# First stage of an attention and two MoE kernel: order of transfers, row tiles, value products and weight conversion rearranged

## The chip, the cores and the metric

The kernel runs on one core of one Trainium2 chip. The metric is the device time of one execution in microseconds (us). PE is TensorE (matrix products), DVE is VectorE, ACT is ScalarE, POOL is GpSimd, and SP is SyncE, which issues nearly all transfers. Each engine works through its own instructions in program order, and waits on semaphores for the others.

## The reference

Three layers in a row on 2304 tokens (4 batches of 576 positions): attention with 8 heads of 64, a first MoE layer with a leaky activation, and a second one with a bounded one. Cut to what is computed:

```python
# attention: q, k, v [4, 8, 576, 64], s [4, 8, 576]
scores = q @ k.T / sqrt(64)
cum = cumsum(maximum(s, 0), axis=-1)
scores = where(causal, -1e9, scores + minimum(-(cum[:, None] - cum[None, :]), 0))
attn = exp(scores - max(scores))
x = (attn / (sum(attn) + 1e-9)) @ v            # [2304, 512] after the heads are joined
# MoE 1: w_in [512, 2048], w_out [2048, 512], alpha [2048]
h = x @ w_in
x = (maximum(h, 0) + alpha * minimum(h, 0)) @ w_out
# MoE 2
h = x @ w_in2
out = (h * clip(h + 3, 0, 6) / 6) @ w_out2
```

Everything is float32. The kernel keeps that precision with products of split values: a high part that PE takes at full rate, and the rest as a second number (names end in h and l, or hi and lo).

## The kernel before

The work stands in one program with three kinds of stages. In the first stage (L663 to L673) PE does attention for the first 256 positions of batches 0 and 1: 16 heads, taken as 8 pairs. In the second (L674 on) it does the first MoE layer for those 512 tokens, one f-step at a time, and between the steps more attention: the first 256 positions of batches 2 and 3, another 8 pairs by the same code. The rest of attention, the rest of MoE 1 and all of MoE 2 come after that.

A head of the first kind has these steps. `scores` (L508) puts products into one PSUM bank, by `softmax_a` (L243): the score products and, for pairs 0 and 1, products that add the running sums of `s` with selection matrices (`pick`, `cum2`). For the other pairs the running sums stand in four extra rows of the operands (`Rows`, L472): the key tile has the sums in its first two rows and ones below, the query tile the reverse, so that one product gives score and bias. DVE then adds the mask and takes the minimum in two passes (L262), ACT takes exponentials (L267), DVE the reciprocal of the sum (L268, L269), and POOL scales (L271). PE transposes the result in three pieces (L518), ACT copies it to SBUF (L519), and PE multiplies it with the values (L525, L526). After each second head ACT and DVE split the outcome into `xhi` and `xlo` (L530, L531), which are MoE 1's input. `attention0` (L533) runs the heads with a lag of one: the transposes of a head come after the scores of the next one.

`cumulate` (L220) makes the running sums: load `s`, scale it on DVE (L227), a scan on DVE that adds a zero tile (L231; POOL fills the zeros, L229), the split (L237, L240), a write to the DRAM tensor `cum_scratch` (L241), from which each pair's four rows are read back (L502, L503). The rows have three pairs of tiles in turn, which POOL fills ahead of time with -1 and 1 (L480, L481).

`keep_clock` (L463) issues products of a constant tile `busy` whose result nobody reads: 18 at the start, and two after the transposes of every head of the first stage.

MoE weights come in eight units of four tiles of 128x512 float32. `load_unit` (L115) issues a unit's transfers from SP. `split_part` (L131) converts: per tile ACT scales (L146), POOL bounds and rounds in two passes (L148, L151), DVE assembles the bits in two passes (L156, L159), ACT copies the high part (L162), DVE subtracts for the low part (L163). `W_LD` and `W_AT` (L28, L29) give the step of attention at which a unit is loaded or converted in the first stage; that conversion has a raised priority (`WP0`). A scheduler places the instructions of each engine by priority, except where `keep_in_program_order` fixes them.

The second stage begins with MoE 1's product h (L186) for f = 0 and 1. ACT and DVE then form the activation (L611 and L612, name gt), its split follows, and two steps later the second product y (L589). There are two PSUM banks for h, so f = 2 waits for the activation of f = 0.

Of the kernel before, what the change touches and what calls it, by code (L numbers as in the profile page):

```python
# [9 lines left out]
F32 = mybir.dt.float32  # L10
# [5 lines left out]
P = 128  # L16
# [11 lines left out]
W_LD = (8, 11, 14)  # L28
W_AT = (2, 14)  # L29
# [31 lines left out]
def attention_moe_moe(ctx, tc, qt, kt, qn, kn, vp, s, w_in1, w_out1, alpha, w_in2, w_out2, out):  # L61
# [158 lines left out]
    def cumulate(pool, first):  # L220

        s_sb = pool.tile([P, S], F32, tag="wcv", bufs=WB0, name="s_sb")
# [18 lines left out]
        nc.sync.dma_start(cum_d.rearrange("t b s -> (t b) s"), cum2[:D].bitcast(F32))  # L241
# [230 lines left out]
    class Rows:  # L472


        def __init__(self, pool, n):
            self.tiles = []
            for i in range(n):
                k = pool.tile([P, 2, NA], F32, name=f"kr{i}")
                q = pool.tile([P, 2, NA], F32, name=f"qr{i}")
                nc.gpsimd.memset(k[:R], -1.0)  # L480
                nc.gpsimd.memset(q[:R], 1.0)  # L481
                self.tiles.append((k, q))

    class Pair:
# [5 lines left out]
        def load(self, pool):  # L490
            i, self.pool = self.i, pool
            if i < 2:
                self.k = pool.tile([P, NA], F32, tag="kraw", name="kraw")
                nc.sync.dma_start(self.k, kn[i, :, :NA])
                self.q = pool.tile([P, NA], F32, tag="qraw", name="qraw")
                nc.sync.dma_start(self.q, qn[i, :, :NA])
            else:
                self.k, self.q = pool.rows.tiles[i % 3]
                both = slice(2 * i, 2 * i + 2)
                nc.sync.dma_start(self.k[R : R + D], kt[both, :D, :NA].rearrange("j d n -> d j n"))  # L500
                nc.sync.dma_start(self.q[R : R + D], qt[both, :D, :NA].rearrange("j d n -> d j n"))
                nc.sync.dma_start(self.k[: R // 2], cum_d[:, both, :NA])  # L502
                nc.sync.dma_start(self.q[R // 2 : R], cum_d[:, both, :NA])  # L503
            self.v = pool.tile([P, 2, 2, D], F32, tag="vraw", bufs=3, name="vraw")
            for j in range(2):
                nc.sync.dma_start(self.v[:, j], vp[2 * i + j, :, :2, :])
# [14 lines left out]
        def values(self, j):  # L521
            if j == 0:
                self.pv = bank("pv")
            js = slice(j * D, (j + 1) * D)
            nc.tensor.matmul(self.pv[js, :NA], self.v[:, j, 0, :], self.pT[j][:, :NA], start=True, stop=False)  # L525
            nc.tensor.matmul(self.pv[js, P:NA], self.v[:, j, 1, :], self.pT[j][:, NA:], start=False, stop=True)  # L526
            if j == 1:
                b, pr = divmod(self.i, H // 2)
                xh, xl = xblock(b)
                nc.scalar.activation(xh[:, pr, :], self.pv[:, :NA], AF.Copy)  # L530
                nc.vector.tensor_tensor(xl[:, pr, :], self.pv[:, :NA], xh[:, pr, :].bitcast(F32), op=ALU.subtract)  # L531

    def attention0(pool, pairs, lag, together):  # L533
# [301 lines left out]
```

## Time and profile before

| what | value |
|---|---|
| median of 3 runs | 1028.53 us (1028.15 to 1029.7) |
| the profiled execution's own time | 1028.13 us |
| its span, first to last instruction | 1026.4 us |
| mean granted TensorE clock | 0.993 of full |
| busy: PE / DVE / ACT / POOL | 1004.1 / 535.6 / 593.6 / 389.0 us |
| end of the first stage on PE, first h product | 53.56 us |

The profile comes from one execution. A busy share is an average over stages, so the stretches matter more than the whole: PE has work nearly all the time from 68 us on, and the gaps lie before that. Idle time of an engine is listed with the instruction whose end released it.

### The profile page before, as it was taken

Reading aid. Unit: us, or ns where it says so; the run is one execution under the profiler, and the core shown is the slowest. Engines: PE = TensorE matmul, PEld = TensorE weight load, DVE = VectorE, ACT = ScalarE, POOL = GpSimd, SP = SyncE. Lnnn points to the kernel's source line nnn. Section 1 sums busy time; section 2 is a strip of 40 time slices with the busy share of each in tenths; the row PEclk is TensorE's granted clock in tenths of the full one; section 3 lists DMA queues with packets and bytes.
Section 4 is the critical chain, followed back from the end, with each engine's and each line's share of the span. In section 5 each row is a group of like instructions: output and inputs, shape, how many; then the busy total and the mean of one; then the engine's idle time right before and its main releaser. Section 6 shows DMA issues by size and latency. Waiting matters only on the chain.

```text
span 1026.4 us, 16686 instructions
## 1 busy us (share of the span) xinstructions
PE 1004.1 (98%) x5858; PEld 866.1 (84%) x5858; DVE 535.6 (52%) x1357; ACT 593.6 (58%) x1326; POOL 389.0 (38%) x535
## 2 busy tenths in 40 slices
PE   6989999999999999999999999999999999999998
PEld 3668878999999999998998888887888888888897
DVE  4669873466666666657644873555322322322222
ACT  4768867678778778778745753665322422422232
POOL 6566737667667666757531630331000000000000
PEclk8999999999999999999999999999999999999999
DMA  5581405113122222222106654000200100000010
GB/s 174 183 288 55 175 4 164 43 39 94 51 85 61 75 63 84 68 78 75 33 27 202 230 201 150 39 0 1 82 1 1 62 1 1 25 17 1 1 42 21
DMA packets 47578, 76.84 MB, mean 75 GB/s; under 512 B 4824, under 2 KB 25480, under 8 KB 47496
## 3 DMA queue, kind: packets, MB, share of 16 engines
q1 hardware_dynamic: 47496, 75.79, 22.7%
q8 instruction: 46, 0.75, 0.3%
q14 instruction: 36, 0.29, 0.1%
HBM read 66.18 MB, written 9.58 MB: 74 GB/s over the span
## 4 chain that ended last, share of the span: by engine, by line
PE 92%; ACT 2%; DVE 2%; DMA 1%; POOL 1%; issue 1%; SPq 0%; ACTq 0%; POOLq 0%; DVEq 0%
PE y L589 19%; PE h L786 19%; PE h L186 19%; PE o L759 13%; PE o L762 6%; PE s L344 4%; PE pv L406 4%; PE pt L381 3%; PE s L256 1%; DMA wraw<-in_w_out 1%; PE pt L518 1%; PE pv L525 1%; ACT t L267 0%; DMA wraw<-in_w_in 0%; DMA qr<-in_qt 0%
## 5 line engine op out<-in xcount | busy, mean ns | idle before, releaser
L186 PE MATMUL h<-xhi,wi 128*128 128x256 f32 (+1 forms) x896 | 225.1, 321 | 2.7 <-DVE gt L612 2.1
L786 PE MATMUL h<-yhl,wi 128*128 128x512 f32 (+1 forms) x960 | 213.2, 370 | 0.2
L786 PEld LDWEIGHTS h<-yhl,wi 128*128 128x128 f32 x960 | 169.3, 188 | 34.7 <-DVE gt L789 1.1
L186 PEld LDWEIGHTS h<-xhi,wi 128*128 128x128 f32 x896 | 155.9, 190 | 16.6 <-DVE gt L612 3.6
L589 PE MATMUL y<-gh,wo 128*128 128x256 f32 (+1 forms) x896 | 166.4, 317 | 0.0
L788 ACT ACTIVATE gt<-h,three 128x512 f32<-128x512 f32 (+1 forms) x80 | 51.7, 646 | 166.9 <-PE h L786 163.3
L789 DVE SCALAR_TENSOR_TENSOR gt<-gt,h 128x512 f32<-128x512 f32 (+1 forms) x80 | 50.7, 634 | 183.7 <-ACT gt L788 183.3
L759 PE MATMUL o<-wo,gh 128*128 128x512 f32 x576 | 145.8, 391 | 0.1
L589 PEld LDWEIGHTS y<-gh,wo 128*128 128x128 f32 x896 | 134.0, 190 | 11.0 <-issue 0.3
L186 PE MATMUL h<-xlo,wi 128*128 128x256 f32 (+1 forms) x448 | 142.2, 318 | 0.0
L759 PEld LDWEIGHTS o<-wo,gh 128*128 128x128 f32 x576 | 106.8, 188 | 22.9 <-ACT gh L792 0.9
L148 POOL TENSOR_SCALAR wcv<-wcv 128x512 f32<-128x512 f32 x64 | 48.8, 767 | 154.5 <-ACT wcv L146 152.9
L589 PE MATMUL y<-gl,wo 128*128 128x256 f32 (+1 forms) x448 | 91.1, 316 | 0.0
L186 PEld LDWEIGHTS h<-xlo,wi 128*128 128x128 f32 x448 | 85.4, 191 | 6.0 <-issue 0.2
L793 DVE TENSOR_TENSOR gl<-gt,gh 128x512 fp32r<-128x512 f32 (+1 forms) x80 | 51.1, 639 | 69.1 <-ACT gh L792 45.5
L356 POOL TENSOR_SCALAR t<-t,rec 128x384 f32<-128x384 f32 (+2 forms) x96 | 65.7, 685 | 53.2 <-DVE rec L355 25.8
L347 DVE CUSTOM_DVE_ANT_0 t<-s,mask 128x384 f32<-128x384 f32 (+2 forms) x96 | 54.0, 564 | 58.4 <-PE pt L381 40.0
L792 ACT ACTIVATE gh<-gt 128x512 fp32r<-128x512 f32 (+1 forms) x80 | 47.2, 591 | 64.0 <-DVE gt L789 32.9
L612 DVE SCALAR_TENSOR_TENSOR gt<-gt,beta,h 128x256 f32<-128x256 f32 (+1 forms) x112 | 61.5, 550 | 40.4 <-ACT gt L611 39.5
L762 PE MATMUL o<-wo,gl 128*128 128x512 f32 x288 | 79.8, 390 | 0.0
L589 PEld LDWEIGHTS y<-gl,wo 128*128 128x128 f32 x448 | 70.1, 190 | 6.2 <-issue 0.2
L352 ACT ACTIVATE t<-t,m 128x384 f32<-128x384 f32 (+2 forms) x96 | 67.2, 700 | 7.2 <-DVE m L347 6.7
(109 smaller groups left out, 1669.4 us busy)
## 6 DMA issues: line engine op xcount, KB each, us to landing
wraw<-in_w_in SPq DMA_DIRECT2D x32, 512.0 KB
wraw<-in_w_out SPq DMA_DIRECT2D x32, 512.0 KB
kraw<-in_kt SPq DMA_DIRECT2D x32, 288.0 KB
qraw<-in_qt SPq DMA_DIRECT2D x32, 160.0 KB
vraw<-in_vp SPq DMA_DIRECT2D x32, 160.0 KB
y_scratch<-yt SPq DMA_DIRECT2D x18, 256.0 KB
yr<-y_scratch SPq DMA_DIRECT2D x4, 1024.0 KB
out<-ot SPq DMA_DIRECT2D x16, 256.0 KB
```

The costliest lines, as they stand in the source:

```text
L186: nc.tensor.matmul(dst, lt, r, start=first and i == 0, stop=last and i == len(terms) - 1)
L347: nc.vector.tensor_tensor_reduce(t[:n, a:e], sc[:n, : e - a], mask[:n, MASK + n - (e - a) :][:, : e - a] if e == w else mask[:n, : e - a], ...
L352: nc.scalar.activation(t[:n, :w], t[:n, :w], AF.Exp, bias=m[-1][:n], scale=-1.0, accum_out=den[:n])
L356: nc.gpsimd.tensor_scalar(t[:n, :w], t[:n, :w], rec[:n], 1.0, op0=ALU.mult, op1=ALU.mult)
L589: nc.tensor.matmul(ys[dc // per][:, o : o + n], which[:, dc * P : (dc + 1) * P], gg, start=(f == 0 and which is wl and dc % per == 0), sto ...
L612: nc.vector.scalar_tensor_tensor(gt, gt, beta[:, f : f + 1], hp[:, :n], op0=ALU.mult, op1=ALU.add)
L759: nc.tensor.matmul(op[i], lt[:, tsl], r, start=(f == 0 and r is wh), stop=False)
L762: nc.tensor.matmul(op[i], gl[:, tsl], wh, start=False, stop=(f == FC - 1))
L786: nc.tensor.matmul(hp[:, :n], lt, r, start=(i == 0), stop=(i == len(terms) - 1))
L788: nc.scalar.activation(gt[:, :n], hp[:, :n], AF.Relu, bias=three)
L789: nc.vector.scalar_tensor_tensor(gt[:, :n], gt[:, :n], 6.0, hp[:, :n], op0=ALU.min, op1=ALU.mult)
L793: nc.vector.tensor_tensor(gl[:, :n], gt[:, :n], gh[:, :n].bitcast(F32), op=ALU.subtract)
```

## The change

- The transfers of the first stage are issued in program order. First come `s`, then keys, queries and values of pairs 0 to 2 and further keys and queries, the write of the running sums, and their rows; weights follow.
- The rows stand in one tile for all six pairs 2 to 7 of the first stage (one tile for the four pair slots of the second), filled on DVE in the first stage and on POOL in the second. Two transfers bring all rows; before there were two for each pair.
- The keys and queries of pairs 0 and 1 share a tile with the weight buffers. The values of a pair come in one transfer, into four buffers in turn instead of three.
- The zero tile is one element that the scan reads again and again. `busy` is filled on DVE.
- `values` does both heads of a pair: four products in the order head 1, head 0 for the first block of keys, then the same for the second.
- The two unread products after the transposes stay for pairs 0 and 1 only: 24 go, 8 stay.
- `W_LD` and `W_AT` put a third unit's conversion into the first stage.

```diff
-W_LD = (8, 11, 14)
-W_AT = (2, 14)
+W_LD = (6, 10, 14)
+W_AT = (2, 8, 14)
...
-            nc.sync.dma_start(s_sb[part * BH : (part + 1) * BH], s)
-        first.load(pool)
+            pin(nc.sync.dma_start(s_sb[part * BH : (part + 1) * BH], s))
+        for pr in first:
+            pr.load(pool, pin)
...
-        zz = pool.tile([P, S], F32, tag="wcv", bufs=WB0, name="zz")
-        nc.gpsimd.memset(zz, 0.0)
+        zero = pool.zero
+        nc.gpsimd.memset(zero, 0.0)
...
-        nc.vector.tensor_tensor_scan(cum, sp, zz, initial=0.0, op0=ALU.add, op1=ALU.add)
+        nc.vector.tensor_tensor_scan(cum, sp, zero.to_broadcast([P, S]), initial=0.0, op0=ALU.add, op1=ALU.add)
...
-        nc.sync.dma_start(cum_d.rearrange("t b s -> (t b) s"), cum2[:D].bitcast(F32))
+        pin(nc.sync.dma_start(cum_d.rearrange("t b s -> (t b) s"), cum2[:D].bitcast(F32)))
+        pool.rows.load(pin)
...
+        def __init__(self, pool, first, n, fill):
+            self.first, self.n = first, n
+            self.k = pool.tile([P, n, 2, NA], F32, name="kr")
+            self.q = pool.tile([P, n, 2, NA], F32, name="qr")
+            fill(self.k[:R], -1.0)
+            fill(self.q[:R], 1.0)
+
+        def load(self, pin=lambda ins: ins):
+            rows = cum_d[:, 2 * self.first : 2 * (self.first + self.n), :NA]
+            for half in (self.k[: R // 2], self.q[R // 2 : R]):
+                pin(nc.sync.dma_start(half.rearrange("r n j k -> r (n j) k"), rows))
...
+        def values(self):
+            pv = bank("pv")
+            for c in range(2):
+                for j in (1, 0):
+                    i = nc.tensor.matmul(
+                        pv[j * D : (j + 1) * D, c * P : NA], self.v[:, j, c, :], self.pT[j][:, c * NA :][:, : NA - c * P],
+                        start=(c == 0), stop=(c == 1),
+                    )
+                    if c == 1 or j == 0:
+                        tc.keep_in_program_order(i)
...
-            if pr.i < H:
+            if pr.i < 2:
                 keep_clock(pr.pool.busy, 2, t)
...
-        nc.gpsimd.memset(pool.busy, 1.0)
-        att = attention0(pool, [Pair(i) for i in range(H)], LAG, 0)
+        nc.vector.memset(pool.busy, 1.0)
+        pool.rows = Rows(ahead, 2, H - 2, nc.vector.memset)
+        att = attention0(pool, [Pair(i) for i in range(H)], LAG)
```

What stands in a row on three engines shows where instructions moved. First SP, from the values of pair 2 on (kr and qr are the row tiles, wraw the weights, cum_scratch the running sums in memory), before:

```order
L506 DMA vraw<-in_vp 128x128 x2
L126 DMA wraw<-in_w_in 128x2x512
L126 DMA wraw<-in_w_out 128x1024
L241 DMA cum_scratch<-cum_109 64x576
L126 DMA wraw<-in_w_in 128x2x512
L126 DMA wraw<-in_w_out 128x1024
L500 DMA kr_111<-in_kt 64x2x256
L501 DMA qr_112<-in_qt 64x2x256
L500 DMA kr_115<-in_kt 64x2x256
L502 DMA kr_119<-cum_scratch 2x2x256
L503 DMA qr_120<-cum_scratch 2x2x256
```

and now:

```order
L510 DMA vraw<-in_vp 128x2x128
L507 DMA kr<-in_kt 64x2x256
L508 DMA qr<-in_qt 64x2x256
L243 DMA cum_scratch<-cum_109 64x576
L507 DMA kr<-in_kt 64x2x256
L508 DMA qr<-in_qt 64x2x256
L488 DMA kr<-cum_scratch 2x12x256
L488 DMA qr<-cum_scratch 2x12x256
L126 DMA wraw<-in_w_in 128x2x512
L126 DMA wraw<-in_w_out 128x1024
```

The four weight transfers stood on both sides of the write; all of them now stand behind the rows.

Then ACT at the start (t are the exponentials of one head in two pieces, wcv the weight tiles), before:

```order
L237 ACTIVATE cum2_109<-cum_163 128x576
L146 ACTIVATE wcv_246<-wraw_238 128x512
L146 ACTIVATE wcv_247<-wraw_240 128x512
L267 ACTIVATE t_191,den_193<-t_191,m_192 128x128
L267 ACTIVATE t_191,den_193<-t_191,m_192 128x256
L267 ACTIVATE t_210,den_212<-t_210,m_211 128x128
L267 ACTIVATE t_210,den_212<-t_210,m_211 128x256
L146 ACTIVATE wcv_264<-wraw_242 128x512
L267 ACTIVATE t_289,den_291<-t_289,m_290 128x128
L267 ACTIVATE t_289,den_291<-t_289,m_290 128x256
L146 ACTIVATE wcv_265<-wraw_244 128x512
L267 ACTIVATE t_320,den_322<-t_320,m_321 128x128
```

and now:

```order
L270 ACTIVATE t_201,den_203<-t_201,m_202 128x128
L270 ACTIVATE t_201,den_203<-t_201,m_202 128x256
L146 ACTIVATE wcv_230<-wraw_222 128x512
L270 ACTIVATE t_273,den_275<-t_273,m_274 128x128
L146 ACTIVATE wcv_231<-wraw_224 128x512
L523 ACTIVATE pT_213<-pt_214 128x384
L270 ACTIVATE t_273,den_275<-t_273,m_274 128x256
L146 ACTIVATE wcv_248<-wraw_226 128x512
L146 ACTIVATE wcv_249<-wraw_228 128x512
L270 ACTIVATE t_301,den_303<-t_301,m_302 128x128
```

The first weight tile stood ahead of the first exponential; it now stands ahead of that of the third head (t_273), and the other three ahead of that of the fourth (t_301).

Last DVE ahead of its first gt, before:

```order
L156 SCALAR_TENSOR_TENSOR wcv_698<-wcv_698,wraw_482 128x512
L159 SCALAR_TENSOR_TENSOR wcv_698<-wraw_482,wcv_698 128x512
L163 TENSOR_TENSOR wo_712<-wcv_698,wo_712 128x512
L262 ISA t_944,m_945<-s_941,mask_86 128x128
L262 ISA m_945 128x1
L262 ISA t_944,m_945<-s_941,mask_86 128x256
L262 ISA m_945 128x1
L612 SCALAR_TENSOR_TENSOR gt_864<-gt_864,beta_82,h_851 128x512
```

and now, in two pieces:

```order
L163 TENSOR_TENSOR wi_687<-wcv_675,wi_687 128x512
L163 TENSOR_TENSOR wo_690<-wcv_676,wo_690 128x512
L265 ISA t_864,m_865<-s_861,mask_86 128x128
L265 ISA m_865 128x1
L265 ISA t_864,m_865<-s_861,mask_86 128x256
L265 ISA m_865 128x1
L538 TENSOR_TENSOR xlo_85<-pv_748,xhi_84 128x256
```

```order
L265 ISA t_1016,m_1017<-s_1013,mask_86 128x128
L265 ISA m_1017 128x1
L265 ISA t_1016,m_1017<-s_1013,mask_86 128x256
L265 ISA m_1017 128x1
L272 RECIPROCAL rec_867<-den_866 128x2
L620 SCALAR_TENSOR_TENSOR gt_824<-gt_824,beta_82,h_811 128x512
```

In both, the last conversion stands ahead of the first gt; before it was the second unit's, now it is the third's. Ahead of gt there was one head's pass of the second stage (t_944) and there are now three (t_864, one more between the pieces, t_1016).

## Rows read from the trace of the kernel before

**Rows 1.** Page, part 1: busy us (share of span), instructions per engine.

```profile
PE 1004.1 (98%) x5858; PEld 866.1 (84%) x5858; DVE 535.6 (52%) x1357; ACT 593.6 (58%) x1326; POOL 389.0 (38%) x535
```

**Rows 2.** By stretch: its length, engines' busy us, granted clock, DMA share.

```profile
11.50:67.10 55.60, 48.53 (x256) 32.36 (x256) 35.27 (x134) 35.41 (x108) 32.14 (x56) 0.91 0.61 208
17.00:26.00 9.00, 6.17 (x21) 4.85 (x22) 7.58 (x33) 6.49 (x23) 8.25 (x14) 0.50 0.36 106
27.00:53.50 26.50, 26.50 (x152) 17.07 (x152) 18.17 (x77) 20.16 (x65) 14.61 (x28) 1.00 0.60 206
60.00:67.90 7.90, 4.91 (x22) 2.68 (x20) 4.76 (x11) 4.09 (x8) 2.28 (x5) 1.00 0.43 117
67.90:72.00 4.10, 4.10 (x11) 3.31 (x12) 3.27 (x11) 4.10 (x13) 3.00 (x6) 0.59 0.91 300
72.00:130.00 58.00, 57.99 (x278) 46.93 (x276) 53.12 (x102) 49.93 (x95) 40.55 (x52) 1.00 0.37 137
130.00:140.00 10.00, 9.27 (x46) 7.09 (x46) 9.72 (x12) 6.61 (x12) 5.42 (x6) 1.00 0.01 2
```

**Rows 3.** Timeline of DVE, 66.3 to 68 us: start, length, instruction.

```profile
67.09 0.75 DVE L612 SCALAR_TENSOR_TENSOR gt<-gt,beta,h 128x512 f32<-128x512 f32 x1 [0.67 <-ACT gt L611]
```

**Rows 4.** Chain that ended last, to 25 us: start, length, what.

```profile
7.90 1.37 DVE cum L231
...
10.78 0.51 SPq L241
...
19.64 0.62 DMA kr<-cum_scratch
```

**Rows 5.** Timeline of SP's issues, 9 to 24 us.

```profile
9.37 0.43 SPq L126 DMA_DIRECT2D wraw<-in_w_in  x1
...
15.54 0.33 SPq L502 DMA_DIRECT2D kr<-cum_scratch  x1
```

**Rows 6.** Timeline of ACT, 12 to 24 us.

```profile
13.70 0.67 ACT L146 ACTIVATE wcv<-wraw 128x512 f32<-128x512 f32 x1 [3.73 <-DMA wraw<-in_w_in]
...
19.95 0.49 ACT L267 ACTIVATE t<-t,m 128x256 f32<-128x256 f32 x1
```

**Rows 7.** POOL by line, 0 to 67.2 us: count, busy us, mean ns.

```profile
L148 POOL TENSOR_SCALAR wcv<-wcv 128x512 f32<-128x512 f32 x10 | 6.1, 613 | 13.9 <-ACT wcv L146 13.4
...
L480 POOL MEMSET kr<- 4x512 f32 x6 | 3.1, 519 | 1.7 <-PE h L468 1.7
```

**Rows 8.** L156, 12 to 67.2 us: ns least/median/most, first and last start.

```profile
L156 DVE SCALAR_TENSOR_TENSOR wcv<-wcv,wraw x8: 682/750/1120, 18.6 to 63.0; 128x512 uint32<-128x512 uint32 x8
```

**Rows 9.** DVE's groups by line, 0 to 67.2 us.

```profile
L262 DVE CUSTOM_DVE_ANT_0 t<-s,mask 128x128 f32<-128x128 f32 (+1 forms) x34 | 10.6, 353 | 8.1 <-PE s L256 4.7 <-POOL t L271 1.8 <-POOL wcv L148 1.6
...
L268 DVE TENSOR_SCALAR den<-den 128x2 f32<-128x2 f32 x16 | 3.2, 202 | 3.6 <-ACT t L267 3.2
```

**Rows 10.** Timeline of PE, 30.5 to 33.5 and 99.3 to 101.2 us.

```profile
30.31 0.50 PE L468 MATMUL h<-t,busy 128*128 128x384 bf16 x2
30.66 0.82 PE L256 MATMUL s<-kr,qr 68*128 68x128 f32 x4
31.31 0.50 PE L468 MATMUL h<-t,busy 128*128 128x384 bf16 x2
31.74 0.65 PE L525 MATMUL pv<-pT,vraw 128*64 128x256 f32 x2
...
32.54 0.55 PE L518 MATMUL pt<-ident,t 128*128 128x128 f32 x3
...
99.79 0.66 PE L525 MATMUL pv<-pT,vraw 128*64 128x256 f32 x4
...
100.60 0.50 PE L589 MATMUL y<-gl,wo 128*128 128x512 f32 x1
```

**Rows 11.** Timeline of DVE and POOL, 48.3 to 51 us.

```profile
48.69 1.05 DVE L156 SCALAR_TENSOR_TENSOR wcv<-wcv,wraw 128x512 uint32<-128x512 uint32 x1
...
48.58 0.62 POOL L148 TENSOR_SCALAR wcv<-wcv 128x512 f32<-128x512 f32 x1
```

More of the change, by code (lines that the diff above doesn't have):

```diff
@@ L472, in attention_moe_moe @@
     class Rows:
[L475 to L482, printed above, removed]
+        def __init__(self, pool, first, n, fill):
[8 more added lines that the diff above has]
+                pin(nc.sync.dma_start(half.rearrange("r n j k -> r (n j) k"), rows))
     class Pair:
@@ L488, in __init__, with load @@
             self.i, self.pT = i, {}
-        def load(self, pool):
+        def load(self, pool, pin=lambda ins: ins):
             i, self.pool = self.i, pool
+            both = slice(2 * i, 2 * i + 2)
             if i < 2:
[L493 to L496, printed above, removed]
-            else:
[L498 to L506, printed above, removed]
+                kq = pool.tile([P, 2, NA], F32, tag="wcv", bufs=WB0, name="kq")
+                self.k, self.q = kq[:, 0], kq[:, 1]
+                pin(nc.sync.dma_start(self.k, kn[i, :, :NA]))
+                pin(nc.sync.dma_start(self.q, qn[i, :, :NA]))
+            else:
+                at = i - pool.rows.first
+                self.k, self.q = pool.rows.k[:, at], pool.rows.q[:, at]
+                pin(nc.sync.dma_start(self.k[R : R + D], kt[both, :D, :NA].rearrange("j d n -> d j n")))
+                pin(nc.sync.dma_start(self.q[R : R + D], qt[both, :D, :NA].rearrange("j d n -> d j n")))
+            self.v = pool.tile([P, 2, 2, D], F32, tag="vraw", bufs=4, name="vraw")
+            pin(nc.sync.dma_start(self.v.rearrange("p j c d -> p j (c d)"), vp[both, :, :2, :].rearrange("j p c d -> p j (c d)")))
         def scores(self, j):
@@ L539, in finish @@
             pr.transpose(j, t)
-            if pr.i < H:
+            if pr.i < 2:
                 keep_clock(pr.pool.busy, 2, t)
-            if len(ready) > together and (not together or j == 0):
-                for _ in range(1 + together):
-                    k, jj = ready.pop(0)
-                    k.values(jj)
-            ready.append((pr, j))
+            if j == 0 and ready:
+                ready.pop(0).values()
+            if j == 1:
+                ready.append(pr)
         loaded = 0
@@ L557, in attention0 @@
             keep_clock(pool.busy, 18)
-            cumulate(pool, pairs[0])
-            loaded = 1
+            cumulate(pool, pairs[:3])
+            loaded = 3
+        else:
+            pool.rows.load()
         ahead(1)
@@ L570, in attention0 @@
             finish()
-        for k, jj in ready:
-            k.values(jj)
+        for pr in ready:
+            pr.values()
     def moe1(w, blocks, gpool, tags, skew):
@@ L667, in attention_moe_moe @@
         pool.pick = ahead.tile([P, 2, BH], F32R, name="pick")
-        pool.rows = Rows(ahead, 3)
-        pool.busy = st.enter_context(tc.tile_pool(name="busy", bufs=1)).tile([P, 512], BF16, name="busy")
-        nc.gpsimd.memset(pool.busy, 1.0)
-        att = attention0(pool, [Pair(i) for i in range(H)], LAG, 0)
+        pool.zero = ahead.tile([P, LINE], F32, name="zero")[:, :1]
+        pool.busy = pool.tile([P, 512], BF16, tag="wcv", bufs=WB0, name="busy")
+        nc.vector.memset(pool.busy, 1.0)
+        pool.rows = Rows(ahead, 2, H - 2, nc.vector.memset)
+        att = attention0(pool, [Pair(i) for i in range(H)], LAG)
         attend(att, 2 * H + 1, pool)
@@ L686, in attention_moe_moe @@
         with ExitStack() as st2:
-            pool2 = Pools(st2, tc, "atta", ("kraw qraw vraw", "t pT"))
-            pool2.rows = Rows(st2.enter_context(tc.tile_pool(name="rows", bufs=1)), 3)
-            att = attention0(pool2, [Pair(i) for i in range(H, H + H // 2)], LAG, 1)
+            pool2 = Pools(st2, tc, "atta", ("vraw", "t pT"))
+            pool2.rows = Rows(st2.enter_context(tc.tile_pool(name="rows", bufs=1)), H, H // 2, nc.gpsimd.memset)
+            att = attention0(pool2, [Pair(i) for i in range(H, H + H // 2)], LAG)
             done = 0
```

20 lines of the change are left out of this document (7 added, 13 removed).

## Prediction

> **What bounds the kernel now.** The page's first part comes first: PE is busy for 1004.1 us [rows 1], of a span of 1026.4. So the table by stretches is next, to find where the other 22 us lie [rows 2] (after the length: busy us of PE, its weight loads, DVE, ACT, POOL). Hold PE's busy time against the length of each stretch: from 27 to 53.5 us and from 72 to 130 us there is no gap; from 17 to 26 us it has 6.17 of 9, at a granted clock of 0.50, the lower of its two levels (1.2 GHz); from 60 to 67.9 us it has 4.91 of 7.9, and the clock is 0.59 for 4 us after that; from 130 to 140 us it has 9.27. All that the change moves of weight lies ahead of 68 us. From 67.09 us, the first DVE step of the first MoE layer [rows 3], PE has work to the end with small gaps. I call the start of that step the gate. The end of the program moves with two things: when the gate opens, and how much PE work is left behind it. PE work saved ahead of the gate gains nothing unless the gate opens earlier too.
>
> What sets the gate? From 11.5 to 67.1 us DVE is busy for 35.27 of 55.6, ACT for 35.41, POOL for 32.14, PE for 48.53 [rows 2]. PE is the fullest: attention goes at PE's pace, and two weight units are converted in the gaps of the other three engines.
>
> The chain of waits tells how the stage starts [rows 4]: the running sum on DVE at 7.90, its write to memory issued at 10.78, and rows of the sum that have landed by 20.26, which the scores of pair 2 wait for. The lists of SP and ACT show the rivalry with the weights: SP issued weights at 9.37 and the first rows at 15.54 [rows 5]; ACT took the first weight tile at 13.70 and the fourth head's last exponential at 19.95 [rows 6].
>
> **The change part by part.**
>
> *Fills on DVE, ahead of the running sum.* Two memsets of 3072 columns and one of 512 now stand first on DVE. No DVE memset is in the trace. A POOL memset of 512 columns took 519 ns, so six of them 3.1 us [rows 7]; DVE took at least 0.68 us for a two-input conversion of 512 columns [rows 8], six of them 4.1; below, nothing excludes half of POOL's price. I take POOL's, the nearest row: 2 x 3.1 + 0.5 = 6.7 us from about 1.3, so DVE is free at 8.0; the scaling of the input (0.7) follows, and the sum starts near 8.7 instead of 7.90, 0.8 us later. The low end gives no delay, the high end 2.8. The wait for POOL's zero tile goes.
>
> The Trainium skill (VectorE: DVE Perf Modes, section "Zero memsets can be issued as uint32 (trn2)") says that a memset takes one cycle per element whatever the type; at that page's 0.96 GHz a large memset is an estimated 3.2 us. No row here shows one on DVE, and by the page the sum would start 0.2 us later than in my count.
>
> *Transfers in a fixed order.* The write goes out at 11.6. The rows follow as two transfers 4.8 us later, as before (10.78 to 15.54 [rows 4, 5]), near 15.3 to 16.4 with what SP has to issue between, and no weight bytes are ahead of them: landed by 18 to 19 rather than 20.26. But the weights leave only now, near 15.4 instead of 9.37. From that issue to ACT's first tile took 4.33 us [rows 5, 6], so conversion begins near 19.7, 6.0 later. In ACT's order the four weight tiles stand ahead of or between the exponentials of heads 2 and 3 (the order of ACT, above): the fourth head's exponential comes at 24 to 25 instead of 19.95. So the early rows are worth little; the chain behind them waits for ACT.
>
> *Less PE work.* Two unread products take 0.35 to 0.43 us of PE (30.31 to 30.66, 31.31 to 31.74 [rows 10]); 24 go, 4.2 us at the lower. One head's values take 0.80 (31.74 to 32.54), two in turn, as the later attention stage has them, 0.81 (99.79 to 100.60) [rows 10]: 8 pairs x 0.79 = 6.3. Together 10.5 us, all ahead of the gate.
>
> *A third unit ahead of the gate.* By the order, DVE has 36 conversion instructions there instead of 24, and the score passes of three heads of the next stage instead of one. That is 12 x 0.70 (between least and median, [rows 8]) = 8.4, two heads' passes at 2 x 0.31 each (10.6 us for 34) and one set of small steps at some 0.37 (202 ns and its successor) = 1.6 [rows 9]: 35.3 + 10.0 = 45.3 us. ACT gains four copies and six scalings, all taken at a scaling's 0.67, and two exponentials of two pieces at 0.5 [rows 6], 8.7: 44.1. POOL gains eight passes of 0.61 [rows 7], 4.9. What hid the conversion before is DVE's 20 us of idle; half of it is now used up.
>
> *Sum.* DVE's first conversion needs a pass on ACT and two on POOL ahead of it: at 21.6 if POOL follows at once (19.7 + 0.67 + 2 x 0.61), at 24.6 if it lags as before (4.9 from 13.70 to 18.6 [rows 6, 8]). I take 23. Between 12.4 and 23 DVE has the first heads' work, 3.6, so it idles for 7.0. With no idle after that, the gate opens at 12.4 + 45.3 + 7.0 = 64.7. With the idle share of 72 to 130 us, where DVE had all the work it could want and still stood for 8% [rows 2], it is 45.3 x 0.08 = 3.6 later, 68.3. I take the middle, 66.5: 0.6 earlier than before. Behind it, less is left: scores of two more heads are done in PE's gaps, 2 x 0.65 (30.66 to 31.31 [rows 10]) = 1.3, and the 0.73 that PE lacked from 130 to 140 go, since the third unit's conversion no longer stands in that stretch. For the clock I allow 0.3 of loss, since PE's gaps are longer ahead of the gate. -0.6 - 1.3 - 0.7 + 0.3 = -2.3 on the profiled run's own 1028.13 (1.73 around its span; 0.4 under the median of 1028.53): **1025.8 us**; 1024.0 with the gate at 64.7, 1027.6 with it at 68.3.
>
> Costed at nothing: values transferred in one piece and one tile for the rows (SP has gaps after 24 us; without them an issue is 0.3 to 0.4 us [rows 5]). POOL's two fills for the next stage, eight times 0.52 = 4.2 us, stand ahead of the scaling of the last heads and wait for pair 7's last score; POOL's 42% of idle hides them, or else they delay the gate by up to 4.2.
>
> **Rivals.** *PE's saving comes through whole.* Attention stays at PE's pace, and the gate moves by 10.5 less some 2 of later start. For it: PE was full from 27 to 53.5 us while DVE had 18.17 of 26.5 [rows 2]. Against it: DVE and ACT then need 45.3 and 44.1 us of the 46 between 12.4 and 58.6. 1028.1 - 8.5 - 1.3 - 0.7 = 1017.6, range 1015 to 1021.
>
> *DVE and POOL stand in each other's way; slower.* At 48.69 a DVE conversion took 1.05 us while a POOL pass ran from 48.58 [rows 11], against 0.68 at least [rows 8]. With 36 conversions packed against 24 POOL passes, 15 stretched by a further 0.37 put the gate at 66.5 + 5.5 = 72.0: +4.9 - 1.7 = +3.2, 1031.3, range 1030.2 to 1035. It decides from a gate at 70.9 on, 12 stretched. For it: the longest conversion, 1.12. Against it: their median is still 0.75, beside a POOL that is 58% busy.
>
> The Trainium skill (SBUF — State Buffer, section "SBUF: two separate sides") has the two engines share a pair of ports that one of them holds for a whole instruction while the other waits. The stretched row agrees in kind. If each of the eight added POOL passes stood fully on DVE's time, 4.9 us, the sum would be 1030.7.
>
> *The clock stays down; slower.* Without the unread products PE has gaps at every head, and after gaps it ran at 0.50 from 17 to 26 us [rows 2]. If it does so for the whole stage, a head's 1.55 us of PE (0.65 scores, 0.5 transposes, 0.4 values) become 3.1, fourteen heads take 43 from 20 us, the MoE's first two steps double too, and the gate opens at 69 to 72: 1029.5 to 1033.
>
> *The wait only moves.* The gate stays at 67 and nothing is gained behind it: 1027.5 to 1029.
>
> **How the numbers follow.** Conversions set the pace: 0.45. PE's saving whole: 0.20. DVE against POOL: 0.17. The clock: 0.12. Moved only: 0.06. What a measurement of this kernel can tell from no change is 0.2%, 2.06 us, so the bound lies at 1026.1 for the profiled run. Of the first case a little over half is faster (0.24), the rest within 0.2% (0.21); of the last two, 0.06 are within. Faster 0.24 + 0.20 = 0.44; same 0.27; slower 0.29. The range of 1017 to 1034 leaves some 0.08 out below and 0.06 above; the first case alone would be 1023.5 to 1028.
>
> **What the profile will show.** If I am right: the running sum on DVE within 1 us of 8.7; ACT's first weight tile at 19 to 20.5; DVE over 85% busy from 23 us to the gate, with PE waiting for DVE or ACT for a quarter of it; the gate at 64.7 to 68.3; PE without gaps from there to 140. A gate at 57 to 60 with PE full is the first rival; conversions with a mean over 0.95, the second; a granted clock of 0.50 over most of 25 to 60 us, the third. I would be wrong most simply if weights issued late took much less or more than 4.3 us, or if DVE's fills don't cost what POOL's do.

## The result: slower by 0.8%, and where it stands in the profile

The changed kernel took 1037.13 us (median of 4 runs, 1036.84 to 1037.85) beside 1029.12 us for the kernel before in the same runs: a ratio of 1.0077, 95% interval 1.0060 to 1.0094. It is slower by 8 us, where 1025.8 was forecast. The profiled execution took 1037.4, its span is 1035.6, 9.2 more than before, and the mean granted clock is 0.979 where it was 0.993.

The page's part 1 after, which answers to [rows 1]:

```profile
PE 1006.5 (97%) x5834; PEld 867.6 (84%) x5834; DVE 552.2 (53%) x1362; ACT 593.4 (57%) x1324; POOL 381.8 (37%) x524
```

PE has 24 products fewer and is busy 2.4 us longer, at a lower mean clock. The table by stretches of after, which answers to [rows 2], says where (length, busy us of PE, its weight loads, DVE, ACT and POOL, granted clock, DMA share, GB/s):

```profile
11.50:78.40 66.90, 54.47 (x236) 36.07 (x235) 48.43 (x155) 42.19 (x124) 41.28 (x63) 0.67 0.61 193
12.00:29.00 17.00, 14.65 (x58) 10.08 (x57) 6.05 (x31) 8.19 (x26) 7.65 (x15) 0.52 0.62 191
29.00:39.50 10.50, 7.71 (x46) 5.22 (x43) 9.97 (x37) 8.27 (x27) 6.67 (x11) 0.97 0.66 229
39.50:67.00 27.50, 22.25 (x80) 14.46 (x81) 22.63 (x62) 17.28 (x53) 23.93 (x34) 0.51 0.66 206
67.00:78.40 11.40, 9.36 (x52) 5.81 (x50) 9.37 (x26) 8.46 (x21) 3.02 (x5) 0.99 0.43 130
130.00:140.00 10.00, 9.69 (x46) 7.53 (x45) 9.66 (x18) 7.82 (x15) 6.62 (x9) 1.00 0.12 34
```

Before, PE was without a gap from 27 to 53.5 us at full clock; now it has 10.50 − 7.71 and 27.50 − 22.25 us of gaps from 29 to 67, and from 39.5 on the lower level of the clock. The gate, the first gt on DVE, moved from 67.09 [rows 3] to 78.43. DVE's timeline of after, some of the instructions around it:

```profile
72.43 0.68 DVE L159 SCALAR_TENSOR_TENSOR wcv<-wraw,wcv 128x512 uint32<-128x512 uint32 x1
73.03 0.68 DVE L163 TENSOR_TENSOR wi<-wcv,wi 128x512 fp32r<-128x512 f32 x1
73.88 0.69 DVE L163 TENSOR_TENSOR wo<-wcv,wo 128x512 fp32r<-128x512 f32 x1 [0.16 <-ACT wo L162]
74.48 0.28 DVE L265 CUSTOM_DVE_ANT_0 t<-s,mask 128x128 f32<-128x128 f32 x1
...
75.04 0.42 DVE L538 TENSOR_TENSOR xlo<-pv,xhi 128x256 fp32r<-128x256 f32 x1
...
78.36 0.16 DVE L272 RECIPROCAL rec<-den 128x2 f32<-128x2 f32 x1
78.43 0.73 DVE L620 SCALAR_TENSOR_TENSOR gt<-gt,beta,h 128x512 f32<-128x512 f32 x1
```

The third unit's last subtractions run at 73.03 and 73.88, then come the score passes of the second stage, and among them the `xlo` of the last pair at 75.04, without which MoE 1's first products can't end. DVE's gt waits for those products, and for ACT's part of it. Rows of PE and ACT after:

```profile
75.75 0.59 PE L186 MATMUL h<-xlo,wi 128*128 128x512 f32 x1
...
77.52 0.58 ACT L619 ACTIVATE gt<-h 128x512 f32<-128x512 f32 x1
```

So the third unit's last steps hold gt by way of `xlo`, PE and ACT: ACT's part ends at 78.10, and DVE's begins 0.33 us later.

An account of the first 200 us serves from here on. Added up over stretches of 1 us, "idle" is the length less PE's busy time, and "clock" is PE's busy time times one minus the granted clock.

| kernel | gate, us | idle | clock | both |
|---|---|---|---|---|
| before | 67.09 | 15.5 | 5.2 | 20.7 |
| after | 78.43 | 20.3 | 18.5 | 38.8 |

That is 18.1 us more lost. PE is busy 2.4 us longer although 13.3 more went to the clock, so by this account its work fell by 10.9; and 2.0 of idle came behind 200 us. 18.1 − 10.9 + 2.0 = 9.2 is the span's 9.2 by construction, no second proof of it. Work was saved as forecast; more was lost than saved.

How the start changed is read from ACT's timeline of after, which answers to [rows 6]:

```profile
15.13 0.49 ACT L270 ACTIVATE t<-t,m 128x256 f32<-128x256 f32 x1
...
20.20 0.66 ACT L146 ACTIVATE wcv<-wraw 128x512 f32<-128x512 f32 x1 [4.49 <-DMA wraw<-in_w_in]
20.77 0.39 ACT L270 ACTIVATE t<-t,m 128x128 f32<-128x128 f32 x1
...
21.45 0.66 ACT L146 ACTIVATE wcv<-wraw 128x512 f32<-128x512 f32 x1 [0.20 <-DMA wraw<-in_w_out]
...
23.74 0.67 ACT L146 ACTIVATE wcv<-wraw 128x512 f32<-128x512 f32 x1 [0.77 <-DMA wraw<-in_w_in]
...
25.14 0.67 ACT L146 ACTIVATE wcv<-wraw 128x512 f32<-128x512 f32 x1 [0.73 <-DMA wraw<-in_w_out]
25.72 0.39 ACT L270 ACTIVATE t<-t,m 128x128 f32<-128x128 f32 x1
```

ACT stands for 4.49 us on a weight tile that has not landed, with the third head's exponentials (20.77) behind it in its list. They had been ready since DVE's last pass for that head, four us before:

```profile
16.57 0.09 DVE L265 DVE_READ_ACCUMULATOR2_ANT m<- 128x1 f32 x1
```

The fourth head's first exponential is at 25.72. The reciprocals of heads 3 to 8 on DVE, the last small step of a head there, began at 20, 21, 24, 26, 30 and 34 us before and at 24, 28, 30, 31, 39 and 40 now.

### The profile page after: what moved, and what is told of

Same layout as the page of the kernel before. It is cut to its first block, busy times and chain, and to the rows that moved or that the text cites. A ratio compares the mean times of both kernels' runs of the same rounds, so it can differ in the third digit from the quotient of the medians.

```text
span 1035.6 us, 16625 instructions
## 1 busy us (share of the span) xinstructions
PE 1006.5 (97%) x5834; PEld 867.6 (84%) x5834; DVE 552.2 (53%) x1362; ACT 593.4 (57%) x1324; POOL 381.8 (37%) x524
## 4 chain that ended last, share of the span: by engine, by line
PE 84%; ACT 6%; DVE 5%; issue 2%; DMA 2%; SPq 1%; POOL 0%; ACTq 0%; POOLq 0%; DVEq 0%
PE h L795 19%; PE y L597 17%; PE h L186 16%; PE o L768 13%; PE o L771 6%; PE s L347 4%; PE pv L409 3%; PE pt L384 3%; DVE wcv L156 1%; DMA wraw<-in_w_out 1%; ACT wraw L154 1%; DVE wcv L159 1%; ACT wcv L146 1%; DVE den L271 1%; DVE t L265 1%
## 5 line engine op out<-in xcount | busy, mean ns | idle before, releaser
L597 PE MATMUL y<-gh,wo 128*128 128x256 f32 (+1 forms) x896 | 163.8, 317 | 0.0
L355 ACT ACTIVATE t<-t,m 128x384 f32<-128x384 f32 (+2 forms) x96 | 67.2, 700 | 16.2 <-DVE m L350 15.2
```

Source lines behind the costliest of these rows:

```text
L355: nc.scalar.activation(t[:n, :w], t[:n, :w], AF.Exp, bias=m[-1][:n], scale=-1.0, accum_out=den[:n])
L597: nc.tensor.matmul(ys[dc // per][:, o : o + n], which[:, dc * P : (dc + 1) * P], gg, start=(f == 0 and which is wl and dc % per == 0), sto ...
```

## The experiments

The theories to tell apart: the unread products that went kept PE's clock up (A); the third unit fills DVE (and ACT, POOL) ahead of the gate (B); weights behind the rows make ACT late (C, or S for the new start as a whole); POOL's two fills of 2048 columns, long ones, block DVE (D); gaps at the start cost the clock (G); each edit makes the scheduler write another order, and that order decides (N).

**Parts undone in the changed kernel.** First the products.

```diff
-            if pr.i < 2:
+            if pr.i < H:
```

> The changed kernel, with the two unread products after the transposes given back to all eight pairs of the first stage. Theory A (the clock): PE ran at 0.50 from 39.6 to 67 us because it had gaps at every head; with the products it stays at 1.00 there, attention's PE pieces halve, and the gate (first gt on DVE, at 80.18) opens at 70 to 74: 1029 to 1032 us. Theory B (conversion ahead of the gate): DVE and ACT set the pace, the clock is a companion; the gate stays within 2 us and the time at 1036 to 1039. Theories C (weights late) and D (long fills) expect the same as B.

1041.47 us, ratio 1.0128 (1.0107 to 1.0150): worse by 4, not better. Idle 23.4, clock 15.6, gate 83.16, against 78.43 in the changed kernel (80.18 above is a misreading). The clock gained 2.9 and PE's work grew by 24 products, but idle rose by 3.1: on balance the products filled no gaps. The removal isn't what cost the time in this kernel.

Then the third unit.

```diff
-W_LD = (6, 10, 14)
-W_AT = (2, 8, 14)
+W_LD = (8, 11, 14)
+W_AT = (2, 14)
```

> The changed kernel with the two lists of steps as before, so that two units, not three, are converted ahead of the gate. Theory B: 12 DVE instructions of 0.70 and their ACT and POOL passes leave; the gate opens at 69 to 72, of which some is given back in 130 to 180 us as before: 1028 to 1031 us. Theory A: PE has even more need of work to keep its clock, the gate gains only 2 to 4: 1033 to 1036 us. Theories C and D expect little: 1035 to 1037.

1038.87, 1.0096 (1.0080 to 1.0112). The gate came forward by 5.1 to 73.31, and the time did not: idle 16.2 (4.1 less), clock 21.3 (2.8 more), and the third unit's conversion came back behind the gate. Not the cause alone.

Weights issued ahead of the sum, among the first transfers (one line, `load_w1(1)`, behind the loads of pairs 0 to 2 in `cumulate`):

```diff
             pr.load(pool, pin)
+        load_w1(1)
```

> The changed kernel with the first unit's four weight transfers issued behind the values of pair 2 and ahead of the write of the running sums, about where they were before the change. Theory C: the first weight tile reaches ACT at 14 to 15 instead of 20.2, the fourth at 19 instead of 25.1, the gate opens 5 to 6 us earlier, 1031 to 1033 us. Theory B: the work ahead of the gate is what counts and the earlier start gives it idle time it can use, 3 to 6 us as well. Theory A: 0 to 2 us, since the clock falls as before.

1048.59, 1.0198 (1.0175 to 1.0220), the slowest of all: the weights took the place of the rows, which left at 19.13 and 19.67; PE stood 3.16 us for them and began the scores of pair 2 at 24.26 instead of 21.15. Three of ACT's four weight tiles now stood ahead of the first exponentials. So giving the weights their early place back and keeping the rest isn't the kernel before.

The edit meant to shorten POOL's fills left the instructions as they were (the trace still has fills of 4x2048). So this run is a repeat of the changed kernel, and shorter fills were not tried:

> The changed kernel with POOL's two fills of 2048 columns for the second stage cut into eight of 512. Theory D: two DVE instructions that took 2.1 us each at 55.7 and 58.0 beside those fills (a reciprocal's input of 2 columns among them, else 0.2) get their turn between the pieces; the gate opens 2 to 4 us earlier, 1033 to 1035 us. The others expect no more than 1 us.

1037.09, 1.0081 (1.0065 to 1.0097). As a repeat it is worth much. The stretch from 30 to 60 us, first in the changed kernel:

```profile
30.00:60.00 30.00, 22.95 (x101) 14.84 (x99) 28.04 (x87) 22.77 (x72) 25.32 (x36) 0.66 0.73 246
```

and in the repeat:

```profile
30.00:60.00 30.00, 28.17 (x103) 18.82 (x101) 25.65 (x87) 22.96 (x72) 24.29 (x35) 0.51 0.68 239
```

The clock was 0.51 against 0.66 and PE's idle time 1.83 against 7.05; the gate stood at 78.47 against 78.43 and the time was equal. In this stretch a low clock eats idle time that PE has anyway. With three units ahead of the gate it goes along with the loss and doesn't set the gate; a run with two units is another matter (below).

Products and third unit undone together:

> The changed kernel with the unread products on all eight pairs and two units as before: of the change the order of transfers, the row tiles with their fills, and values in turn stay. Theory S: this order is the cause, so nothing is won back: 1034 to 1040 us, with a gate after 72. Theory A and B together: with both undone the gate is at 62 to 67 and the time 1022 to 1029 us.

1040.88, 1.0122 (1.0102 to 1.0142): gate 78.38, idle 24.8, clock 13.7. With the weights early as well:

> The changed kernel with four parts undone at once: products on all eight pairs, two units, the first unit's weights ahead of the write of the sums, and POOL's fills in pieces of 512. What stays is values in turn, one tile of rows and fills on DVE. Theory S: with the weights early the stage is that of the values run, 1027 to 1031 us. If no part by itself is the cause, but the order of instructions that comes out of each edit: anything from 1030 to 1045 us.

1032.90, 1.0041 (1.0024 to 1.0058), gate 69.69. (The fills named there stayed as they were here too.) What was left of the change, values, tiles and DVE's fills with its fixed order of transfers, cost 4 us here, and here the rows were again behind the weights.

**Parts done alone in the kernel before.** Third unit, the same edit the other way:

> The kernel before with the changed two lists of steps alone: a third unit's conversion ahead of the gate. Theory B (that conversion is the cause): gate at 74 to 78 instead of 67.09, 1033 to 1037 us. Theory S (the cause is the new start: weights issued at 14.4 instead of 9.37 and the exponentials of heads 2 and 3 behind them): here the start is the old one, so PE's full attention hides the work, 1027 to 1031 us.

1040.33, 1.0120 (1.0102 to 1.0138): the whole loss and more from the two tables alone. The heads are on time here; the stretch from 60 to 90 us holds the loss:

```profile
60.00:90.00 30.00, 23.01 (x79) 16.61 (x78) 24.27 (x55) 18.21 (x41) 15.21 (x25) 0.72 0.54 186
```

PE has 7 us of gaps there and a clock of 0.72. On DVE the unit's last subtractions end ahead of gt, at 74.89:

```profile
72.15 0.69 DVE L163 TENSOR_TENSOR wi<-wcv,wi 128x512 fp32r<-128x512 f32 x1
72.76 0.68 DVE L163 TENSOR_TENSOR wo<-wcv,wo 128x512 fp32r<-128x512 f32 x1
...
74.89 0.75 DVE L612 SCALAR_TENSOR_TENSOR gt<-gt,beta,h 128x512 f32<-128x512 f32 x1 [0.28 <-ACT gt L611]
```

The 24 products alone (`if pr.i < 2`):

> The kernel before without the 24 unread products of pairs 2 to 7. If they are only load on a full PE, 4 to 5 us go from PE and the time is 1024 to 1026 us. Theory A (their removal lets the clock fall): PE has gaps, the granted clock is 0.50 over a good part of 30 to 60 us, and the time is 1030 to 1036 us. Theory S: the clock falls only where PE waits anyway, 1025 to 1029 us.

1031.72, 1.0028 (1.0016 to 1.0040). Less work, more time: idle 22.0 (6.5 more), clock 6.6, gate 69.08. Values of two heads in turn alone (`values` and `finish` as after):

> The kernel before with the changed values function alone (both heads of a pair in turn, one step later). PE's work ahead of the gate falls by 6.3 us. If PE sets the pace there, as the prediction's first rival has it: 1022 to 1025 us. If DVE and ACT take over soon: 1026 to 1028 us. Theory A: the gaps that PE then has lower its clock, 1029 to 1034 us.

1029.74, 1.0015 (1.0003 to 1.0026). PE's work fell by 7.5 by the account and the gate opened 2.8 earlier, at 64.31, but idle rose by 5.2 (and 1.6 behind 200 us) and the clock's loss by 2.6.

Rows first, alone: the write of the sums and then the rows of pair 2 pinned ahead of the weights, the tiles of rows as before.

```diff
+                pin = tc.keep_in_program_order if i == 2 else (lambda ins: ins)
-                nc.sync.dma_start(self.k[: R // 2], cum_d[:, both, :NA])
-                nc.sync.dma_start(self.q[R // 2 : R], cum_d[:, both, :NA])
+                pin(nc.sync.dma_start(self.k[: R // 2], cum_d[:, both, :NA]))
+                pin(nc.sync.dma_start(self.q[R // 2 : R], cum_d[:, both, :NA]))
```

> The kernel before with the change's order of first transfers alone: the write of the running sums and the rows of pair 2 are held ahead of the first unit's weights; fills, values, products and units as before. Theory S (the weights behind the rows are the cause): the first weight tile on ACT at 18 to 20 instead of 13.70, gate at 71 to 76, 1033 to 1039 us. If the order of transfers costs nothing by itself: the rows are there 2 to 3 us earlier, gate at 65 to 67, 1025 to 1029 us.

**1021.49, 0.9932 (0.9909 to 0.9954)**: a gain of 7 us. The weights leave at 14.80, as late as after (14.41). ACT's timeline of this kernel:

```profile
15.44 0.40 ACT L267 ACTIVATE t<-t,m 128x128 f32<-128x128 f32 x1 [0.24 <-DVE m L262]
...
18.42 0.66 ACT L146 ACTIVATE wcv<-wraw 128x512 f32<-128x512 f32 x1 [2.00 <-DMA wraw<-in_w_in]
18.98 0.39 ACT L267 ACTIVATE t<-t,m 128x128 f32<-128x128 f32 x1
...
20.61 0.65 ACT L146 ACTIVATE wcv<-wraw 128x512 f32<-128x512 f32 x1
```

Three heads' exponentials stand ahead of the first weight tile, and several more between the tiles. So weights issued this late do no harm by themselves. In the changed kernel ready work stands behind them in ACT's list; PE's clock differs as well, 0.91 here from 12 to 30 us and 0.53 there.

**Is it the order that the scheduler draws anew?** One start product fewer, or two more, change little work:

```diff
-            keep_clock(pool.busy, 18)
+            keep_clock(pool.busy, 17)
```

> The kernel before with 17 instead of 18 unread products at the start: 0.36 us of PE less, in a stretch in which PE then waits for the running sum anyway. The work is the same, but the scheduler writes another order (DVE's list differs in 410 lines). Theory N (the order that comes out decides, and each edit draws a new one): the time moves by 2 to 10 us. If not, it stays within 1 us of before: 1027.5 to 1029.5 us.

> The kernel before with 20 instead of 18 unread products at the start: 0.7 us of PE more, of which some 0.1 to 0.7 lie ahead of the first scores. Theory N: the time moves by 2 to 10 us. If not: 1028 to 1029.5 us.

With 17: 1027.94, 0.9991 (0.9979 to 1.0003); with 20: 1029.39, 1.0012 (1.0000 to 1.0023). This doesn't test N: by line and tile name only 4 and 6 of DVE's 1357 instructions stand elsewhere in these traces than before. In fewer products, values, third unit and rows first, each alone, it is some 380 to 980. What a new order by itself is worth is not shown; a loss as small as that of values alone may be no more than that.

**Third unit and fewer products on the kernel with rows first**, and the start gap by itself (`nc.vector.memset(pool.busy, 1.0)` there, which leaves PE waiting from 7.85 to 10.42 us):

> The kernel of the rows_first run with the change's lists of steps, so that a third unit is converted ahead of the gate. Theory B (as on the kernel before, where it cost 12 us): 1029 to 1035 us, gate past 70 with DVE at the third unit until shortly ahead of it. If the earlier rows make room for it: 1020 to 1024 us.

> The kernel of the rows_first run without the 24 unread products of pairs 2 to 7. As on the kernel before (3.4 us slower): 1023 to 1027 us. If they are only load: 1017 to 1020 us.

> The kernel of the rows_first run with one edit: DVE instead of POOL fills the tile of the unread products, so that these start at 1.4 instead of 5.1 us, end near 8, and leave PE idle until the first scores at 11.6. Theory G: the clock is at 0.50 from 12 to some 28 us, and the time goes from 1021.5 to 1026 to 1032 us. If the start doesn't matter: within 2 us of 1021.5.

Third unit: 1033.48, 1.0045 (1.0032 to 1.0058). Fewer products: 1026.57, 0.9971 (0.9959 to 0.9983). Gap: **1020.44, 0.9922 (0.9898 to 0.9946)**, the fastest here, and faster than both kernels of this case. So this gap costs nothing here. But it is shorter than the changed kernel's (2.57 us against 3.68; 2.97 with two units), and the clock was at 0.50 for some 7 us, not for the 16 that G forecast: for the changed kernel this run doesn't answer G. Its stretches:

```profile
12.00:30.00 18.00, 16.50 (x82) 12.03 (x82) 10.32 (x51) 12.54 (x43) 11.65 (x20) 0.81 0.56 183
30.00:60.00 30.00, 29.41 (x160) 19.42 (x158) 22.21 (x78) 21.62 (x66) 20.96 (x36) 1.00 0.72 258
60.00:90.00 30.00, 29.26 (x139) 23.84 (x140) 23.98 (x53) 24.43 (x51) 17.55 (x26) 1.00 0.48 168
```

From 30 to 90 us PE lacks 1.3 us; its gate is at 60.76, its account 9.3 idle and 3.4 clock. The same with the one-element zero tile, filled early:

> The kernel of the b10 run (rows first, tile of the unread products filled on DVE) with the change's one-element zero for the running sum, which then needn't wait for POOL: the sum starts near 5.4 instead of 7.9, the first scores at 9 instead of 11.6, and PE, which waited 2.6 us for them, is fed: 1017 to 1020 us. If the weights set the pace of the heads instead: 1020 to 1022 us, as b10.

1023.21, 0.9952 (0.9937 to 0.9968). The sum starts 2 us sooner, and nothing is gained over the last.

**The start of the changed kernel.** With 30 start products the scheduler puts four heads' exponentials ahead of all weight tiles on ACT. The same edit shortens PE's gap ahead of the first scores from 3.68 to 1.83 us and raises its clock, so it is no test of ACT's order alone. With two units instead of three besides, the third unit and the slow start are both gone:

```diff
-            keep_clock(pool.busy, 18)
+            keep_clock(pool.busy, 30)
```

> The changed kernel with 30 instead of 18 unread products at the start, so that PE is busy from 1.3 until the first scores at 11.7. Theory G (the gap at the start lets the clock fall, and the first heads then run at half speed): the clock stays at 1.00 past 12 us, the loss of clock in 12 to 30 us falls from 7.4 us to under 3, the fourth head's exponential comes 3 to 5 us earlier, 1030 to 1034 us. If the third unit or the missing products set the time: 1035 to 1038 us.

> The changed kernel with two units as before and with 30 unread products at the start, by which the scheduler puts the first four heads' exponentials ahead of all weight tiles on ACT. Each of the two alone left the time at 1039 us. If both causes have to go: heads at the pace of the rows_first run (fourth reciprocal near 20, last near 50), gate at 62 to 66, 1022 to 1029 us. If something else in the changed kernel costs (row tiles, fills, shared buffers): 1033 us or more.

With 30 alone: 1039.67, 1.0098 (1.0076 to 1.0120). The reciprocals of heads 3 to 8 begin at 19, 20, 24, 27, 29 and 30 us, on time, but the third unit's last subtraction is at 73.59 and the gate at 77.53, after 2.62 us in which DVE waited for ACT's part of gt. With both: 1027.65, **0.9990 (0.9978 to 1.0003)**, gate 66.51, idle 16.1, clock 9.8: the loss is gone, with the fewer products, the values and the tiles still in place.

| changed kernel | ACT's order | clock, 12 to 30 us | units | gate, us | ratio |
|---|---|---|---|---|---|
| as it is | weights ahead | 0.53 | 3 | 78.43 | 1.0077 |
| two units | weights ahead | 0.50 | 2 | 73.31 | 1.0096 |
| 30 start products | heads ahead | 0.81 | 3 | 77.53 | 1.0098 |
| both | heads ahead | 0.81 | 2 | 66.51 | 0.9990 |

Two causes, the third unit and the slow start, each enough to hold the gate at 73 us or later; that is why neither showed when it was taken away alone. What in the start does it is not settled between ACT's order and PE's clock, and with two units the traces speak for the clock. The stretch from 12 to 52 us, with two units and then with both:

```profile
12.00:52.00 40.00, 38.79 (x146) 26.79 (x146) 21.57 (x100) 24.54 (x78) 19.43 (x37) 0.51 0.60 200
```

```profile
12.00:52.00 40.00, 33.33 (x177) 23.20 (x176) 27.91 (x115) 28.12 (x94) 29.20 (x46) 0.79 0.76 264
```

With two units alone PE is busy for 38.79 of the 40 us at 0.51 and gets through 146 products instead of 177. Between the two runs the idle account hardly moves (16.2 and 16.1), and the clock's goes from 21.3 to 9.8: the whole gain. The clock had fallen by 11 us, before ACT began to stand for its first weight tile, at 16.84. What kept it low, no run shows.

By ratios, in us at 1028.5, the parts alone cost: rows first −7.0, third unit +12.3 (on top of rows first 1.0045 − 0.9932, +11.6), fewer products +2.9 (+4.0), values +1.5. Their sum is 9.7, against 8 for the whole change; that it comes near is luck, since the table shows that the parts don't add up.

## Why the prediction was wrong

- *The sum for the gate* is the step that failed: 66.5 forecast, 78.43 measured. From 11.5 us on it was 45.3 us of DVE's work and 9.7 of idle. Measured were 48.43 and 66.90 − 48.43 = 18.47: 3.1 of work, 8.8 of idle more, together the 11.9 us. The start was near: DVE's first conversion came at 24.21 (23 forecast). From there DVE stood for 9.7 of 54.2 us, 18%, where the sum allowed 1.8, or 3.6 at its upper end. Of the 3.1 more work some 2.5 are instructions stretched beside POOL's two fills (DVE is busy from 55.69 to 60.03 with five that elsewhere take 1.9); the rest of the work was right. The idle share was taken from 72 to 130 us. The stretch ahead of the gate would have warned: before, DVE stood there for a third of the time (16.4 of 48.5 us from 18.6 on), and with the third unit alone for 13.7 of 56.4. There each conversion hops between ACT, POOL and DVE in lists that also carry the heads, and PE waits for both. PE's longest waits after, 24.2 to 78.4 us (total, times, longest):

```profile
PE s L259 <- DVE m L265: 6.3, 6, 2.0
...
PE h L186 <- DVE xlo L538: 2.7, 2, 2.4
...
PE pv L529 <- ACT pT L523: 1.9, 3, 0.6
```

  ACT's timeline of after shows the hops near the end:

```profile
66.84 0.63 ACT L162 ACTIVATE wi<-wcv 128x512 fp32r<-128x512 f32 x1 [0.94 <-DVE wcv L159]
...
69.62 0.63 ACT L162 ACTIVATE wo<-wcv 128x512 fp32r<-128x512 f32 x1 [1.06 <-DVE wcv L159]
70.16 0.37 ACT L537 ACTIVATE xhi<-pv 128x256 fp32r<-128x256 f32 x1
...
72.28 0.64 ACT L162 ACTIVATE wi<-wcv 128x512 fp32r<-128x512 f32 x1 [0.99 <-DVE wcv L159]
73.21 0.63 ACT L162 ACTIVATE wo<-wcv 128x512 fp32r<-128x512 f32 x1 [0.30 <-DVE wcv L159]
73.75 0.37 ACT L537 ACTIVATE xhi<-pv 128x256 fp32r<-128x256 f32 x1
```

  The copies wait for DVE, and `xhi`, which PE needs, stands behind them. The idle after the first conversion ("8%", 3.6 us) is the term that was mis-sized, and "I take the middle" can't mend that, for both ends lay below 70. How much of the 9.7 us is the third unit and how much the slow start is not shown. The sign that DVE would be over 85% busy from 23 us to the gate came out at 82%, 45.65 of 55.43 us: conversions did fill DVE, the sum left too little beside them.
- *Transfers in a fixed order.* Rows issued at 13.74 (15.3 forecast), weights at 14.41 (15.4), ACT's first tile at 20.20 (19.7), the fourth head's exponentials at 25.72 and 26.48 (24 to 25): all near, the first tile by luck, since its transfer took 5.79 us and not 4.33, and left 1.0 earlier. But "the early rows are worth little" was wrong: alone, with ACT's list and the clock at the start in a better state, they gain 7 us. And the late heads, seen on paper, were charged to DVE's first conversion alone, not to the heads that stand behind them: heads 7 and 8 were 9 and 6 us late by their reciprocals.
- *Fills on DVE.* Right. The fill and the next stand 3.20 us apart (3.1 forecast), the sum starts at 8.28 (8.7). DVE's timeline of after:

```profile
1.97 2.62 DVE L482 MEMSET kr<- 4x3072 f32 x1 [0.58 <-issue]
5.17 2.62 DVE L483 MEMSET qr<- 4x3072 f32 x1 [0.59 <-DMA s_sb<-in_s]
...
8.28 1.36 DVE L233 TENSOR_TENSOR_SCAN cum<-sp,zero 128x576 f32<-128x576 f32 x1
```

  The Trainium skill's one cycle per element (VectorE: DVE Perf Modes, section "Zero memsets can be issued as uint32 (trn2)") gave an estimated 3.2 us, and the start-to-start time agrees, as does the time from the end of the first fill (4.59) to that of the second (7.79). The rows show 2.62 of it as busy; the profile puts the 0.59 between them down to the arrival of `s`, though in other runs with the same 0.59 it names no such wait.
- *Less PE work*: 10.5 forecast, 10.9 measured by the account. The rule that such a saving gains nothing unless the gate opens earlier held, and more: fewer products alone cost 2.9 us, values alone 1.5, though there the gate did open 2.8 earlier.
- *Behind the gate* −2.0 (with 0.3 for the clock −1.7) was forecast; the gate moved by 11.3 and the span by 9.2, so −2.1. PE is busy 9.69 of 10 us from 130 to 140, where it was 9.27. But the gate is not the whole measure: from it to the last instruction the runs above take between 957 us (the changed kernel) and 964 us (values alone).
- *Rivals.* "The clock stays down" named what the profile shows, 0.50 over most of 25 to 60 us, but its time fell short (1029.5 to 1033). Its reason, the missing unread products, fails: giving them back made it worse. With three units the repeat shows the same gate at two levels of the clock; with two, PE was full at 0.51, so there the clock is the likeliest limit. "PE's saving whole" didn't happen here. "DVE against POOL" came nearest in time (1030.2 to 1035, still short), but wanted conversions with a mean over 0.95 us; those of L156 and L159 took 0.85 and 0.86. But DVE's two-column step took 2.14 us beside POOL's fill of 1.79; by the rows of DVE and POOL in the changed kernel,

```profile
55.69 2.14 DVE L271 TENSOR_SCALAR den<-den 128x2 f32<-128x2 f32 x1
...
56.01 1.79 POOL L482 MEMSET kr<- 4x2048 f32 x1
```

  so DVE stands beside these fills, at two places of some 2 us, both 18 us and more ahead of the gate. They don't make the loss: the third unit in the kernel before has only fills of 512 columns ahead of its gate at 74.89, and the run with 30 start products and two units has fills of 2048 (at 46.61 and 48.35) without the loss. What they cost in the changed kernel stays open. The Trainium skill (SBUF — State Buffer, section "SBUF: two separate sides") has one of the two engines hold the shared ports for a whole instruction while the other waits, for DVE instructions in a 2-port mode among others. This row agrees in kind, DVE's step ending at 57.83 and POOL's fill at 57.80; whether the step runs in such a mode no row tells.
- *The range*, 1017 to 1034, ended 3 us too low: each rival on the slow side moved the gate by one mechanism alone, and none let the third unit and the slow start come together. The third unit by itself costs 11 to 12 us on two kernels, and no rival asked for that.

## What to carry to other kernels

When work is moved ahead of a gate into "idle" engines, follow it in each engine's own list: count the hops between engines, and take the idle share from the stretch it goes into, not from one where the engine has a choice. In the rows-first run weights issued 5 us later did no harm, with ready work ahead of their first user; look for the instruction that waits for data and for what it holds up. An edit that moves two things, as the start products did with ACT's order and the clock, settles neither; and whether a run tests the order of instructions is read from the orders in the traces. Where two causes may each hold the same point, take them away together as well as one by one, and read lost time as PE's idle time and its clock together, since the one can hide in the other.

## What the runs showed of the hardware

- PE at work without a pause can stay at the lower level. In the changed kernel, by stretches:

```profile
12.00:22.00 10.00, 10.00 (x42) 7.60 (x40) 2.40 (x16) 3.57 (x12) 2.28 (x5) 0.53 0.85 284
22.00:29.00 7.00, 4.66 (x18) 2.48 (x17) 3.65 (x15) 4.62 (x15) 5.38 (x10) 0.50 0.29 57
```

  For 10 us PE was busy throughout, some 7 of them with products over 64 or 68 rows, at 0.53; the full clock came between 29 and 30 us, after a stretch with gaps. No run here tells what raised it.
- Less work on PE made the kernel slower twice (fewer products with and without rows first, 4.0 and 2.9 us; values alone, 1.5, is too near the spread to count): idle time and the clock's loss together rose by more than the work fell, 9.2 us against 5.1 and 7.9 against 3.9.
- The changed kernel's program lost 8.0 and 13.9 us to the clock from 30 to 60 us in two executions and took the same time.
